# Cross-quadrant maxima by a TensorE transpose in some attention units, and side work of VectorE placed elsewhere

## The chip, the cores and the metric

One core of a Trainium2 chip. The metric is the device time of one execution in microseconds. The engines are called as the profile calls them: PE (TensorE matmul) with PEld (its weight loads), DVE (VectorE), ACT (ScalarE), POOL (GpSimd), SP (the queue that issues most DMAs).

## The reference

```python
x = A_x                                              # [1, 2048, 576]
sa, ca, ga, sb, cb, gb = (silu(c) @ w_mod) in six rows of 576
h = layernorm(x) * (1 + ca) + sa
q = (h @ wq) in 32 heads of 128                      # k, v: the last 512 cached keys, 16 heads, each used by 2 query heads
p = softmax(q @ k.T * 128**-0.5)
x = x + ga * ((p @ v) @ wo)
h = layernorm(x) * (1 + cb) + sb
x = x + gb * ((relu(h @ W_gate) * (h @ W_up)) @ W_down)   # 4608 hidden columns
```

All in float32. The kernel makes every large product out of two fp32r pieces per operand (a rounded "hi" and a remainder "lo"): hi*hi, hi*lo and lo*hi, so three matmuls for one.

## The kernel before

The program has two parts. The first, to about 1570 us, is attention in 128 **units**: one unit is one query head with one block of 512 queries (`UNITS` lists them; a key/value head `g` is visited for some query blocks after another). The second part is the gated MLP, with a seven-product scheme in place of eight; the change leaves it as it is.

The order of the instructions of PE, DVE, ACT and POOL is the order in which Python issues them (`manual_schedule`), and each engine works its list strictly in that order. The loop over `u` at the end of the function writes a unit out by hand. Around it stands a table `sched` of side steps, each with a time `10*u + k`: `run(u, k)` issues all steps up to that time, at place `k` of unit `u`. With such steps the layer norms of later query blocks, the loading and splitting of weights, the sums that make the six modulation rows, and the preparation of the MLP are spread over the units.

What one unit `u` does, in the order in which it stands:

- `s_half` (L543 to L545): 12 matmuls of keys times queries, 512 wide, into two PSUM tiles `s`. The third matmul of each group reads `qlo`, the low part of the projected queries. Behind each half DVE reduces the tile (`t`, L548): the largest score in every 32x32 block, transposed on the way.
- `max_pre` and `sum_pre` (L553, L558) bring the unit's maxima and the previous unit's sums of exponentials into a small tile `mxs`, 32 columns, where each of the four groups of 32 partitions ("quadrants") holds its own part.
- `turn`: the four quadrants are joined. Three DVE moves copy quadrants 1 to 3 to the first (L562, `mxs`), two reductions take the maximum and the sum over the four (L570), three moves copy the result back (L562, `both`).
- `qproj(u + 1)` (L467): 14 matmuls, the projection of the next unit's queries, into PSUM `qps`. A layer norm's transposes (L397, `lta` and `ltb`) may stand ahead of it.
- `max_bc` (L587): a DVE transpose spreads the maxima over 512 columns (`mb`); then `sum_inv` takes the reciprocal of the sums.
- `piece` (L683, `wo`): 12 matmuls of 288 columns of the output projection, into the one tile of the pool `psW`. A layer norm's transposes use the same tile, and DVE or ACT reads them out of it (L449, L443, L409).
- `pv_half(u - 1, 0)`, `exp_half` (DVE subtracts `mb` from `s`, L600; ACT takes exponentials and rounds, `hi`; POOL starts the sums, `ks` L606), `sum_bc(u - 1)` (L582, `rb`), `q_lo(u + 1)` (L525), `ksum_op` (`ks`: L618 on DVE, then L618 on POOL), `pv_half(u - 1, 1)`, another `piece`, `o_mul(u - 1)` (L664), and on POOL `lo_half` twice (`lo`, L612), which the next unit's `pv` needs.

The pool `psM` has two banks, given out in turn to `qps`, `pv` and a few transposes and sums. The pool `psS` has two tiles for `s`.

Side steps that the change touches are made by `prep(name, t, pr, gap)`: a load (`.l`) at an earlier place; for the output weights a gating (`.g`: DVE multiplies 128x576 weights by a modulation row, L264, both operands in SBUF); and the last step (`.c`) at `t`: the split into hi and lo, or, for the modulation rows, one multiply-add on DVE (`mod_step`, L120 and L122, `macc`).

Of the kernel before, what the change touches and what calls it, by code (L numbers as in the profile page):

```python
# [7 lines left out]
F32 = mybir.dt.float32  # L8
# [3 lines left out]
ALU = mybir.AluOpType  # L12
AX = mybir.AxisListType

P = 128
# [9 lines left out]
SCALE = float(P) ** -0.5  # L25
H2 = D // 2
SUM, MLP0 = 3, 8
NLAST = 5


@with_exitstack
def kernel(
# [13 lines left out]
    nc = tc.nc  # L46
# [10 lines left out]
    bp = ctx.enter_context(tc.tile_pool(name="bp", bufs=3))  # L57
    op = ctx.enter_context(tc.tile_pool(name="op", bufs=3))
# [6 lines left out]
    psM = psM_scope.__enter__()  # L65
# [3 lines left out]
    ident = cp.tile([P, P], F32, name="ident")  # L69
# [9 lines left out]
    mxs = cp.tile([P, 4, 32], F32, name="mxs")  # L79
    nc.vector.memset(mxs, 0.0)  # L80
    both = cp.tile([P, 32], F32, name="both")
# [52 lines left out]
    def prep_mod(j, t):  # L134
        st = {}

        def load():
            st["raw"] = xp.tile([P, 640], F32, tag="xm", name=f"wm{j}_{t}")
            nc.sync.dma_start(st["raw"][:, :D], wmod[j, :, t * D:(t + 1) * D])

        return load, lambda: mod_step(j, t, st["raw"][:, :D])
# [350 lines left out]
    NU = HKV * NQB * 2  # L492
# [3 lines left out]
    VIS = [(g, qbs) for qbs in ((0, 1), (2, 3)) for g in range(2)]  # L496
    VIS += [(g, (0, 1, 2, 3)) for g in range(2, HKV - NLAST)]
    VIS += [(g, (0, 1)) for g in range(HKV - NLAST, HKV)] + [(g, (2, 3)) for g in range(HKV - NLAST, HKV)]
    UNITS = [(g, qb, 2 * g + hh) for g, qbs in VIS for qb in qbs for hh in range(2)]
# [5 lines left out]
    def unit(u):  # L505
        return UNITS[u]
# [16 lines left out]
    def q_lo(u):  # L523
        qlo[u] = qp.tile([P, 512], F32R, tag="qlo", name=f"qlo{u}")
        nc.vector.scalar_tensor_tensor(qlo[u], qst.pop(u)[0], SCALE, qhi[u].bitcast(F32),  # L525
                                       op0=ALU.mult, op1=ALU.subtract)

    st_, t4, pt, hi_, lo_, bc, rb, rinv, ks_, pvps, done, o = ({} for _ in range(12))

    def by_sum(u):  # L530
        return 0 <= u < SUM
# [23 lines left out]
    def sum_pre(u):  # L555
        if by_sum(u):
            return
        nc.vector.tensor_reduce(mxs[:, 0, 16:], ks_.pop(u).rearrange("p (b j) -> p b j", j=32),  # L558
                                axis=AX.X, op=ALU.add, apply_transpose=True)

    def shift(dst, src):
        nc.vector.tensor_reduce(dst, src[:, :, None], axis=AX.X, op=ALU.max)  # L562

    def turn(u):
        for q in range(1, 4):
            shift(mxs[:32, q, :], mxs[32 * q:32 * q + 32, 0, :])
        for j, op in ((0, ALU.max), (1, ALU.add)):
            if u > SUM if j else u < NU:
                c = slice(16 * j, 16 * j + 16)
                nc.vector.tensor_reduce(both[:32, c], mxs[:32, :, c].rearrange("p q b -> p b q"),  # L570
                                        axis=AX.X, op=op)
        for q in range(1, 4):
            shift(both[32 * q:32 * q + 32, :], both[:32, :])

    def sum_inv(u):
        r = rinv[u] = sp.tile([P, 16], F32, tag="ri", name=f"ri{u}", bufs=1)
        nc.vector.reciprocal(r, both[:, 16:])
# [5 lines left out]
                            r[:, :, None].to_broadcast([P, 16, 32]))  # L583

    def max_bc(u):
        m = bp.tile([P, 512], F32, tag="bc", name=f"mb{u}")
        nc.vector.transpose(m.rearrange("p (b j) -> p b j", j=32),  # L587
                            both[:, :16, None].to_broadcast([P, 16, 32]))
        if u > SUM:
            sum_inv(u - 1)  # L590
        bc[u] = m
# [5 lines left out]
    def exp_half(u, h):  # L597
        t = st_.pop((u, h))
        p = pp.tile([P, 2, 512], F32, tag="p", name=f"p{u}_{h}")
        nc.vector.tensor_tensor(p, t, bc[u][:, None, :].to_broadcast([P, 2, 512]),  # L600
                                op=ALU.subtract)
        nc.scalar.activation(p, p, AF.Exp, bias=0.0, scale=1.0)  # L602
        pt[u, h] = p
        if h == 0 and not by_sum(u):
            ks_[u] = xp.tile([P, 512], F32, tag="xm", name=f"ks{u}")
            nc.gpsimd.tensor_tensor(ks_[u], p[:, 0, :], p[:, 1, :], op=ALU.add)  # L606
        if h and u:
            hi_half(u, 0)
# [11 lines left out]
    def pv_half(u, h, late=False):  # L620
        g, qb, hd = unit(u)
        if h == 0:
            pvps[u] = psM.tile([P, 512], F32, tag="mm", name=f"pv{u}")
        ps, v, a, b = pvps[u], vs[g], hi_[u, h], lo_[u, h]
        for j in range(2):
            kt = 2 * h + j
            nc.tensor.matmul(ps, v[:, kt, :], a[:, j, :], start=(kt == 0), stop=False)  # L627
            nc.tensor.matmul(ps, v[:, 4 + kt, :], a[:, j, :], start=False, stop=False)  # L628
            if not late:
                nc.tensor.matmul(ps, v[:, kt, :], b[:, j, :], start=False, stop=(kt == 3))  # L630
        for j in range(2 if late else 0):
            kt = 2 * h + j
            nc.tensor.matmul(ps, v[:, kt, :], b[:, j, :], start=False, stop=(kt == 3))
        if h:
            done[u] = pvps.pop(u)
# [707 lines left out]
    def step(name, t, fn, *args):  # L1343
        sched.append((t, len(sched), fn, args))
# [4 lines left out]
    def hook(q):  # L1349
        return 10 * (q // 4) + HOOK[q % 4]  # L1350

    def prep(name, t, pr, gap=2):
        q = 4 * (t // 10) + HOOK.index(t % 10)
        step(name + ".l", hook(q - gap), pr[0])
        if len(pr) > 2:
            step(name + ".g", t if t == 49 else hook(q - 1), pr[1])
        step(name + ".c", t, pr[-1])

    def setd(d, k, fn):
        def go():  # L1360
# [155 lines left out]
    for t, key, d, k in ((5, ("q", 0), wqs, 0), (8, ("k", 0), ks, 0), (12, ("q", 1), wqs, 1),  # L1516
                         (16, ("v", 0), vs, 0), (37, ("o", 0), wos, 0), (43, ("o", 1), wos, 1)):
        sk(t, key, d, k)
    live = {"q": wqs, "k": ks, "v": vs, "o": wos}
    early = range(HKV - NLAST + 1, HKV)  # L1520
    parks = {c: [w for g in early for w in weights(g, {x: {} for x in "qkvo"}) if w[0][0] in c]
             for c in ("q", "kv", "o")}
    seen, first = {0}, HKV - NLAST + 2
    for i in range(1, len(VIS)):
# [12 lines left out]
        seen.add(g)  # L1537
    for i in range(1, HKV - NLAST):
        B = 80 * i
        for c, t, gap, a in (("q", 16, 5, 0), ("kv", 24, 5, 1), ("o", 44, 6, 2)):  # L1540
            if parks[c] and i > a:
                key, d, pr = parks[c].pop(0)
# [1 line left out]
                sk(B + t + 9, key, d, key[1])  # L1544
    assert not any(parks.values())
    for i in range(15):
        prep(f"m{3 + i // 5}.{i % 5}", 109 + 30 * i - 10 * (i == 8), prep_mod(3 + i // 5, i % 5), 5)
    step("m3.pad", 238, mod_pad, 3)
    step("m4.pad", 388, mod_pad, 4)
    step("m3.col", 250, setd(mods, "b0", lambda: mod_col(3, 0.0)()))  # L1550
# [39 lines left out]
    for i in range(4):  # L1590
        m = 2 + 2 * i
# [79 lines left out]
    mlp = mlp_slots()  # L1671

    def last_unit():
        sum_inv(NU - 1)
        sum_bc(NU - 1)
        o_mul(NU - 1)
# [21 lines left out]
    t = 546  # L1698
    for s in ("P1", "P2", "P4", "P7", "P5", "P6", "P3"):
        for xx in range(2):  # L1700
            for fn in w_later(s, xx, (xp, "xm", 640)):
                step("w.l", t, fn)
                t = after(t + 8)
# [40 lines left out]
    def run(u, k):  # L1744
        t = 10 * u + k
        while sched and sched[-1][0] <= t:
            fn, args = sched.pop()[2:]
            fn(*args)
# [11 lines left out]
    for u in range(NU):  # L1760
        run(u, 0)
        if u > 1 and u % 2 == 0:
            o_hi(u - 2)
            o_lo(u - 2)
        s_half(u, 0)
        s_half(u, 1)
        max_pre(u)
        if u:
            sum_pre(u - 1)
        turn(u)  # L1770
        run(u, 1)
        if u + 1 < NU:
            qproj(u + 1, 0, 14)
        else:
            piece(at[10 * u + 1])
        if u == 1:
            hi_half(0, 0)
            hi_half(0, 1)
            lo_half(0, 0)
            lo_half(0, 1)  # L1780
        run(u, 2)
        if u + 1 == NU:
            pv_half(u - 1, 0, True)
        max_bc(u)
        if u + 1 < NU:
            q_hi(u + 1)
        run(u, 3)
        if 10 * u + 3 in at:
            piece(at[10 * u + 3])
        if u > 1 and u % 2:  # L1790
            o_hi(u - 2)
            o_lo(u - 2)
        run(u, 4)
        if by_sum(u - 1):
            pv_sums(u - 1)
        elif u + 1 == NU:
            pv_half(u - 1, 1, True)
        elif u:
            pv_half(u - 1, 0)
        flush(pend_act)  # L1800
        exp_half(u, 0)
        flush()
        run(u, 5)
        if u == 0:
            q_lo(1)
        exp_half(u, 1)
        if u > SUM:
            sum_bc(u - 1)
        if 0 < u < NU - 1:
            q_lo(u + 1)  # L1810
        if by_sum(u - 1):
            sums_inv(u - 1)
        ksum_op(u, 0)
        ksum_op(u, 1)
        run(u, 6)
        if SUM < u < NU - 1:
            pv_half(u - 1, 1)
        if 10 * u + 6 in at:
            piece(at[10 * u + 6])
        run(u, 7)  # L1820
        if u:
            o_mul(u - 1)
        flush()
        run(u, 8)
        if u + 1 == NU:
            flush(pend_act)
        if u:
            hi_half(u, 1)
        flush(pend_act)
        if u:  # L1830
            lo_half(u, 0)
            lo_half(u, 1)
        run(u, 9)
# [56 lines left out]
```

## Time and profile before

| | |
|---|---|
| median of 3 runs | 2844.81 us (2843.04 to 2846.78) |
| the profiled execution | 2843.61 us, its span 2841.8 us |
| PE busy | 2812.6 us, 99% of the span, 15054 matmuls |
| DVE busy | 2321.3 us, 82% |
| POOL busy | 2216.8 us, 78% |
| ACT busy | 1415.6 us, 50% |

The share of busy time hides stages: DVE is at 92% while attention runs and at 61% to 81% afterwards. PE's busy time is that of pipelined matmuls, whose ends are modelled, so a row's length is not what it costs: the distance to the next row's start is. An idle time in front of a matmul is shown with what ended it. A weight load is issued ahead of its matmul, so the same wait also shows, a little longer, in the rows of PEld.

### The profile page before, as it was taken

What the parts mean: (1) busy time and instruction counts of PE and PEld (TensorE: products, weight loads), DVE (VectorE), ACT (ScalarE), POOL (GpSimd) and SP (SyncE); (2) the same over time, 40 slices, a digit from 0 to 9 for tenths busy, and PEclk for the clock granted to TensorE, in tenths of its full rate; (3) what the DMA queues carried; (4) which work ended last, traced back from release to release, by engine and by line L of the source; (5) the groups of instructions that cost most, each with busy time, mean ns of one, the idle gap of its engine ahead of it and who ended that gap; (6) DMA issues with size and microseconds to landing.
All of it is one profiled execution on the core that took longest, in us unless ns stands there. A gap on an engine that the chain in (4) does not pass through costs nothing.

```text
span 2841.8 us, 42016 instructions
## 1 busy us (share of the span) xinstructions
PE 2812.6 (99%) x15054; PEld 2451.2 (86%) x15054; DVE 2321.3 (82%) x3866; ACT 1415.6 (50%) x2020; POOL 2216.8 (78%) x1596
## 2 busy tenths in 40 slices
PE   8999999999999999999999999999999999999999
PEld 7788888888888888888888888888888888888888
DVE  8999999999989999888999877778777566666666
ACT  6766666666666666666656433333333222222220
POOL 6878888888899989777778766777887577777773
PEclk9999999999999999999999999999999999999999
DMA  6322132223232223322244465666777844444443
GB/s 236 106 91 89 62 101 91 85 68 110 101 103 86 93 63 136 99 76 79 73 139 138 151 210 204 228 230 224 259 252 278 316 156 155 156 156 153 151 150 137
DMA packets 166881, 411.43 MB, mean 145 GB/s; under 512 B 15728, under 2 KB 62576, under 8 KB 166672
## 3 DMA queue, kind: packets, MB, share of 16 engines
q1 hardware_dynamic: 132768, 287.65, 31.4%
q10 hardware_dynamic: 33904, 121.09, 10.8%
q8 instruction: 119, 1.95, 0.3%
q14 instruction: 90, 0.74, 0.1%
HBM read 276.53 MB, written 160.73 MB: 154 GB/s over the span
## 4 chain that ended last, share of the span: by engine, by line
PE 64%; DVE 5%; POOL 2%; ACT 1%; issue 1%; DMA 0%; SPq 0%; ACTq 0%; POOLq 0%; DVEq 0%
PE gh_P L1159 28%; PE md L683 9%; PE mf L767 6%; PE wo L683 6%; PE qps L467 5%; PE s L545 2%; PE s L544 2%; PE s L543 2%; PE pv L630 1%; PE pv L628 1%; PE pv L627 1%; DVE t L548 1%; POOL lo L612 1%; POOL ks L606 1%; DVE p L600 1%
## 5 line engine op out<-in xcount | busy, mean ns | idle before, releaser
L612 POOL TENSOR_TENSOR lo<-p,hi 128x1024 fp32r<-128x1024 f32 x256 | 623.1, 2455 | 0.5
L1159 PE MATMUL gh_P<-hop_B,wop 128*128 128x512 f32 x1470 | 352.9, 390 | 0.0
L548 DVE TRANSPOSE_TENSOR_REDUCE t<-s 128x32 f32<-128x1024 f32 x256 | 311.9, 1235 | 42.1 <-PE s L545 34.7
L1159 PEld LDWEIGHTS gh_P<-hop_B,wop 128*128 128x128 f32 x1470 | 270.0, 188 | 50.6 <-DVE q L1196 0.2
L600 DVE TENSOR_TENSOR p<-s,mb 128x1024 f32<-128x1024 f32 x256 | 299.9, 1209 | 0.3
L602 ACT ACTIVATE p<-p 128x1024 f32<-128x1024 f32 x256 | 264.1, 1056 | 58.8 <-DVE p L600 57.1
L467 PE MATMUL qps<-hTa,wA 128*128 128x512 f32 x1176 | 281.8, 390 | 1.8 <-DVE hTa L443 1.4
L1159 PE MATMUL gh_P<-hop_T,wop 128*128 128x512 f32 x1138 | 282.8, 390 | 0.0
L683 PE MATMUL wo<-woga,ohi 128*128 128x288 f32 x1344 | 271.9, 295 | 5.0 <-DVE hTa L449 3.9
L467 PEld LDWEIGHTS qps<-hTa,wA 128*128 128x128 f32 x1176 | 220.2, 188 | 49.0 <-DVE hTa L443 1.8
L595 ACT CAST hi<-p 128x1024 fp32r<-128x1024 f32 x256 | 257.2, 1039 | 0.0
L683 PE MATMUL md<-wogb,hhi 128*128 128x288 f32 x1280 | 257.2, 294 | 0.0
L618 POOL TENSOR_TENSOR ks<-ks,p 128x512 f32<-128x512 f32 x125 | 166.8, 1334 | 107.3 <-DVE ks L618 104.4
L1159 PEld LDWEIGHTS gh_P<-hop_T,wop 128*128 128x128 f32 x1138 | 208.8, 188 | 39.3
L683 PEld LDWEIGHTS wo<-woga,ohi 128*128 128x128 f32 x1344 | 224.3, 188 | 20.3 <-DVE hTa L449 5.6
L521 ACT ACTIVATE qhi<-qps 128x512 fp32r<-128x512 f32 x128 | 76.4, 597 | 330.8 <-PE qps L467 327.5
L606 POOL TENSOR_TENSOR ks<-p 128x512 f32<-128x512 f32 x125 | 162.4, 1299 | 100.9 <-ACT p L602 99.2
L683 PEld LDWEIGHTS md<-wogb,hhi 128*128 128x128 f32 x1280 | 212.2, 188 | 10.6 <-DVE q L1184 0.2
L694 DVE TENSOR_TENSOR acc<-md,acc 128x576 f32<-128x576 f32 x160 | 120.1, 754 | 104.7 <-PE md L683 103.4
L1159 PE MATMUL gh_P<-hy_T,wop 128*128 128x512 f32 x618 | 200.6, 391 | 0.0
L683 PE MATMUL wo<-woga,olo 128*128 128x288 f32 x672 | 198.7, 296 | 0.4 <-POOL olo L672 0.3
L672 POOL TENSOR_TENSOR olo<-rb,ohi 128x512 fp32r<-128x512 f32 x128 | 166.6, 1302 | 32.2 <-ACT ohi L668 31.9
(322 smaller groups left out, 7510.3 us busy)
## 6 DMA issues: line engine op xcount, KB each, us to landing
wop<-wk_P SPq DMA_DIRECT2D x133, 640.0 KB
wk_P<-wop ACTq DMA_DIRECT2D x119, 640.0 KB
wr<-wlay SPq DMA_DIRECT2D x68, 384.0 KB
againq<-akq SPq DMA_DIRECT2D x22, 640.0 KB
againo<-ako SPq DMA_DIRECT2D x18, 576.0 KB
rogb<-wd SPq DMA_DIRECT2D x36, 288.0 KB
rwA<-wq SPq DMA_DIRECT2D x32, 320.0 KB
roga<-wo SPq DMA_DIRECT2D x32, 288.0 KB
```

The costliest lines, as they stand in the source:

```text
L467: return [lambda i=i, a=a, b=b: nc.tensor.matmul(ps, a, b, start=(i == 0), stop=(i == n - 1)) for i, (a, b) in enumerate(ops)]
L548: nc.vector.tensor_reduce(t4[u][:, 2 * h:2 * h + 2, :].rearrange("p k b -> p (k b)"), t.rearrange("p k (b j) -> p (k b) j", j=32), axis=AX ...
L595: nc.scalar.copy(hi_[u, h], pt[u, h])
L600: nc.vector.tensor_tensor(p, t, bc[u][:, None, :].to_broadcast([P, 2, 512]), op=ALU.subtract)
L602: nc.scalar.activation(p, p, AF.Exp, bias=0.0, scale=1.0)
L606: nc.gpsimd.tensor_tensor(ks_[u], p[:, 0, :], p[:, 1, :], op=ALU.add)
L612: nc.gpsimd.tensor_sub(lo_[u, h], pt[u, h], hi_[u, h].bitcast(F32))
L618: eng.tensor_tensor(ks_[u], ks_[u], pt[u, 1][:, j, :], op=ALU.add)
L672: nc.gpsimd.tensor_sub(olo[u], o.pop(u), ohi[u].bitcast(F32))
L683: nc.tensor.matmul(ps[:, half, :H2], a[:, sl], w[b][:, cs], start=(n == 0 and seed is None), stop=(n == 5), skip_group_check=seed is not None)
L767: nc.tensor.matmul(ps[:, j, :H2], x[:, sl], w[:, c:c + H2], start=i == 0, stop=i == 2)
L1159: nc.tensor.matmul(ps, a, c, start=s not in ("P2", "P3") and i == 0, stop=i == len(ops) - 1, skip_group_check=True)
```

## The change

- A unit with `u < 15` or `u >= 110` (`by_turn`, and the closing step of the last unit) joins the quadrants in another way. DVE makes one transpose of the 32 columns, repeated four times, inside each quadrant (`mt`, 128x128, in the first columns of the tile that later holds `mb`); PE transposes that 128x128 tile through the identity into a PSUM tile `qm` (`spread`, right behind the projection of the next unit and ahead of the first `piece`); DVE reduces `qm` over the quadrants, once for the maxima and once for the sums (`quads`). The eight small operations of `join` are gone there. `qm` is a third tile in the rotation of `psM`. The other 95 units keep `join`.
- In every unit `q_lo(u + 1)` now stands ahead of `sum_bc(u - 1)`, with a place 5.5 between them for side steps.
- All gatings but one (`t == 49`) and the 15 multiply-adds of the modulation rows move to that place 5.5.

```diff
+TURNS = (15, 110)
...
+    def by_turn(u):
+        return u < TURNS[0] or u >= TURNS[1]
...
-    def turn(u):
+    def join(u):
         for q in range(1, 4):
             shift(mxs[:32, q, :], mxs[32 * q:32 * q + 32, 0, :])
...
+    def turn(u):
+        if not by_turn(u):
+            join(u)
+            return
+        bps[u] = psM.tile([P, 512], F32, tag="mm", name=f"qm{u}")
+        bc[u] = bp.tile([P, 512], F32, tag="bc", name=f"mb{u}")
+        mt[u] = bc[u][:, :P]
+        nc.vector.transpose(mt[u].rearrange("p (a b) -> p a b", a=4),
+                            mxs[:, 0, None, :].to_broadcast([P, 4, 32]))
+
+    def spread(u):
+        if not by_turn(u):
+            return
+        nc.tensor.transpose(bps[u][:, :P], mt.pop(u), ident)
+
+    def quads(u, k):
+        return bps[u][:, :P].rearrange("p (a k b) -> p k b a", a=4, k=2)[:, k]
+
+    def sum_add(u):
+        if by_turn(u + 1):
+            nc.vector.tensor_reduce(both[:, 16:], quads(u + 1, 1), axis=AX.X, op=ALU.add)
...
     def max_bc(u):
-        m = bp.tile([P, 512], F32, tag="bc", name=f"mb{u}")
+        if by_turn(u):
+            nc.vector.tensor_reduce(both[:, :16], quads(u, 0), axis=AX.X, op=ALU.max)
+        if u > SUM:
+            sum_add(u - 1)
+        m = bc[u] if by_turn(u) else bp.tile([P, 512], F32, tag="bc", name=f"mb{u}")
...
-            step(name + ".g", t if t == 49 else hook(q - 1), pr[1])
-        step(name + ".c", t, pr[-1])
+            step(name + ".g", t if t == 49 else (t - 6) // 10 * 10 + 5.5, pr[1])
+        step(name + ".c", t + shift, pr[-1])
...
-        prep(f"m{3 + i // 5}.{i % 5}", 109 + 30 * i - 10 * (i == 8), prep_mod(3 + i // 5, i % 5), 5)
+        prep(f"m{3 + i // 5}.{i % 5}", 109 + 30 * i - 10 * (i == 8), prep_mod(3 + i // 5, i % 5), 5, -3.5)
...
     def last_unit():
+        spread(NU)
+        sum_add(NU - 1)
         sum_inv(NU - 1)
...
             pv_half(u - 1, 0, True)
+        spread(u)
         max_bc(u)
...
         exp_half(u, 1)
+        if 0 < u < NU - 1:
+            q_lo(u + 1)
+        run(u, 5.5)
         if u > SUM:
             sum_bc(u - 1)
-        if 0 < u < NU - 1:
-            q_lo(u + 1)
```

Three places show it. First DVE in unit 7, one in which a layer norm's transposes are read out (`hTa`); before:

```order
L548 TENSOR_REDUCE t_7_1604<-s_1_1606 128x32
L553 TENSOR_REDUCE mxs<-t_7_1604 128x16
L558 TENSOR_REDUCE mxs<-ks_1545 128x16
L562 TENSOR_REDUCE mxs<-mxs 32x32 x3
L570 TENSOR_REDUCE both<-mxs 32x16 x2
L562 TENSOR_REDUCE both<-both 32x32 x3
L449 TENSOR_TENSOR hTa_4_1634<-lta_0_1624,hTa_0_1633 128x512
L587 STREAM_TRANSPOSE mb_1660<-both 128x512
```

and now:

```order
L549 TENSOR_REDUCE t_7_1583<-s_1_1585 128x32
L554 TENSOR_REDUCE mxs<-t_7_1583 128x16
L559 TENSOR_REDUCE mxs<-ks_1524 128x16
L586 STREAM_TRANSPOSE mb_1596<-mxs 128x128
L450 TENSOR_TENSOR hTa_4_1608<-lta_0_1598,hTa_0_1607 128x512
L613 TENSOR_REDUCE both<-qm_1595 128x16
L599 TENSOR_REDUCE both<-qm_1595 128x16
L617 STREAM_TRANSPOSE mb_1596<-both 128x512
```

Eight small operations stood between the reductions of the scores and the reading of the norm's transposes; one transpose stands there now, and the two reductions of `qm` come behind.

Second PE in the same unit, from the end of the projection of the next unit's queries (now; before, the row of `qm` is not there and all else is the same):

```order
L468 MATMUL qps_1618<-hTa_7_1461,againq_1254 128x512
L468 MATMUL qps_1618<-hTa_8_1407,againq_1254 128x512 x2
L592 MATMUL qm_1595<-ident,mb_1596 128x128
L713 MATMUL wo_3_1642<-woga_1014,ohi_1117 128x288 x2
L713 MATMUL wo_3_1642<-woga_1014,olo_1119 128x288
```

One transpose stands between the projection and the output projection's piece, and it reads what DVE writes into `mb`.

Third DVE in unit 43, the one place where a gating and a multiply-add fell together (`p_1` is the second half of the scores less the maxima); before:

```order
L600 TENSOR_TENSOR p_1_6320<-s_1_6244,mb_6277 128x1024
L582 STREAM_TRANSPOSE rb_6325<-ri_6279 128x512
L525 SCALAR_TENSOR_TENSOR qlo_6327<-qps_6262,qhi_6281 128x512
L618 TENSOR_TENSOR ks_6318<-ks_6318,p_1_6320 128x512
L664 TENSOR_TENSOR rb_6325<-pv_6305,rb_6325 128x512
L122 SCALAR_TENSOR_TENSOR macc_5977<-wm_1_6201,sT,macc_5977 128x576
L264 TENSOR_TENSOR roga_6232<-roga_6232,mrow_1005 128x576
L548 TENSOR_REDUCE t_44_6374<-s_0_6367 128x32
```

and now:

```order
L630 TENSOR_TENSOR p_1_6275<-s_1_6199,mb_6232 128x1024
L526 SCALAR_TENSOR_TENSOR qlo_6280<-qps_6217,qhi_6236 128x512
L265 TENSOR_TENSOR roga_6188<-roga_6188,mrow_992 128x576
L123 SCALAR_TENSOR_TENSOR macc_5896<-wm_1_6157,sT,macc_5896 128x576
L608 STREAM_TRANSPOSE rb_6284<-ri_6234 128x512
L648 TENSOR_TENSOR ks_6273<-ks_6273,p_1_6275 128x512
L694 TENSOR_TENSOR rb_6284<-pv_6260,rb_6284 128x512
L549 TENSOR_REDUCE t_44_6329<-s_0_6322 128x32
```

Both side operations moved from behind `o_mul` (the second `rb` row), just ahead of the next unit's `t`, to a place behind `qlo` and ahead of the first `rb`, `ks` and `o_mul`.

More of the change, by code (lines that the diff above doesn't have):

```diff
@@ L526, in q_lo @@
                                        op0=ALU.mult, op1=ALU.subtract)
-    st_, t4, pt, hi_, lo_, bc, rb, rinv, ks_, pvps, done, o = ({} for _ in range(12))
+    st_, t4, mt, pt, hi_, lo_, bc, rb, rinv, ks_, pvps, done, o, bps = ({} for _ in range(14))
     def by_sum(u):
@@ L1350, in hook, with prep @@
         return 10 * (q // 4) + HOOK[q % 4]
-    def prep(name, t, pr, gap=2):
+    def prep(name, t, pr, gap=2, shift=0):
         q = 4 * (t // 10) + HOOK.index(t % 10)
```

## Prediction

> **What bounds the kernel now.** I read the page's first part, then stages by time, then who PE's weight loads wait for in each stage, and last single units in order of time. The sum is made against the profiled execution, 2843.6 us, 1.2 us (0.04%) under the median of the runs.
>
> ```profile
> PE 2812.6 (99%) x15054; PEld 2451.2 (86%) x15054; DVE 2321.3 (82%) x3866; ACT 1415.6 (50%) x2020; POOL 2216.8 (78%) x1596
> ```
>
> Busy time, per engine. PE is the bound; what can be won are the stretches in which it waits. The next view cuts the span (columns: length, then busy time and instructions of PE, PEld, DVE, ACT, POOL, granted clock, DMA share, GB/s): units 0 to 14, 15 to 109, 110 to 126.
>
> ```profile
> 24.35:219.47 195.12, 183.73 (x923) 154.39 (x924) 178.71 (x348) 131.47 (x184) 157.11 (x105) 0.98 0.34 119
> 219.47:1357.32 1137.85, 1132.69 (x5916) 980.26 (x5915) 1039.42 (x1951) 766.83 (x1048) 975.61 (x598) 1.00 0.28 91
> 1357.32:1570.44 213.12, 208.33 (x1096) 178.39 (x1095) 201.59 (x386) 135.19 (x183) 168.31 (x104) 1.00 0.37 121
> ```
>
> PE idles 11.4 us in the first stage, 5.2 and 4.8 in the next two; DVE is at 91% to 95% in all three. The change touches hardly anything behind them. Who PE's weight loads waited for, first stage, then second, then third (total, times, longest):
>
> ```profile
> PEld wo L683 <- DVE hTa L449: 5.6, 4, 2.4
> PEld sums L643 <- ACT woga L218: 2.6, 1, 2.6
> PEld s L545 <- DVE qlo L525: 2.0, 3, 1.3
> PEld qps L467 <- DVE hTa L443: 1.8, 1, 1.8
> ...
> PEld s L545 <- DVE qlo L525: 8.6, 17, 2.0
> PEld s L543 <- DVE p L600: 1.2, 1, 1.2
> ...
> PEld wo L683 <- DVE lfb L409: 4.4, 4, 1.1
> PEld s L545 <- DVE qlo L525: 3.5, 5, 1.6
> ```
>
> Nearly all are waits for something that DVE does late. A load runs ahead of its matmul, so of each a part is not lost: a wait of 1.1 us there stands below as one of 0.67 at the matmul, which with about 0.27 for refilling PE costs 0.94. I take 0.15 off each. Now a unit without a stall (unit 9), PE then DVE:
>
> ```profile
> 150.75 3.34 PE L467 MATMUL qps<-hTa,againq 128*128 128x512 f32 x14
> 153.93 0.42 PE L683 MATMUL wo<-woga,ohi 128*128 128x288 f32 x2
> ...
> 149.59 2.61 DVE L548 TRANSPOSE_TENSOR_REDUCE t<-s 128x32 f32<-128x1024 f32 x2 [0.63 <-PE s L545]
> 152.24 0.27 DVE L553 TENSOR_REDUCE mxs<-t 128x16 f32<-128x64 f32 x1
> 152.43 0.70 DVE L558 TRANSPOSE_TENSOR_REDUCE mxs<-ks 128x16 f32<-128x512 f32 x1
> 153.16 0.55 DVE L562 TENSOR_REDUCE mxs<-mxs 32x32 f32<-32x32 f32 x3
> 154.22 0.56 DVE L562 TENSOR_REDUCE both<-both 32x32 f32<-32x32 f32 x3
> 154.82 0.71 DVE L587 STREAM_TRANSPOSE mb<-both 128x512 f32<-128x512 f32 x1
> 161.42 2.61 DVE L548 TRANSPOSE_TENSOR_REDUCE t<-s 128x32 f32<-128x1024 f32 x2 [0.50 <-PE s L545]
> ```
>
> A clean unit takes 11.83 us (161.42 less 149.59). The join takes DVE 1.66 us, from 153.16 to 154.82.
>
> **The change, part by part.** *The new join.* The transpose inside the quadrants is not in the trace. Its bounds are a 32x32 move, 0.18 us (0.55 for three), and the 512-wide transpose, 0.71; it has a quarter of the latter's columns, so I take 0.22. It would end at 153.38, and PE leaves the projection at 153.93: in a clean unit PE does not wait, with 0.55 us to spare. PE then transposes, its end and a semaphore take some 0.3 us, two reductions (64 elements per partition as at L553, bounds 0.18 and 0.27 each) 0.5: `mb` starts at about 154.8, as before. So the chain of a clean unit is no shorter; DVE has 0.9 us less to do and waits for PE instead. What gains are things queued behind the join.
>
> *PE's own cost.* Eight transposes of a norm:
>
> ```profile
> 1397.90 1.03 PE L397 MATMUL ltb<-ident,xnb 128*128 128x128 f32 x8
> 1398.69 1.17 PE L467 MATMUL qps<-hTa,againq 128*128 128x512 f32 x4
> ```
>
> 0.79 us from start to start, 0.10 each, and a little for the change of shape: 0.115 for one alone, 34 of them: **+3.9 us**. Nothing hides it.
>
> *Units 113 to 117 and 5 to 8, a norm read out behind the join:*
>
> ```profile
> 1401.96 0.81 DVE L409 TENSOR_SCALAR lfb<-ltb,mcol,mcol 128x512 f32<-128x512 f32 x1
> 1402.82 0.53 PE L683 MATMUL wo<-againo,ohi 128*128 128x288 f32 x2 [0.67 <-DVE lfb L409]
> ```
>
> The piece needs the PSUM tile that `lfb` reads. `lfb` comes 1.44 us earlier (1.66 less 0.22), more than the 0.67. Each of the four late ones cost 0.67 and about 0.27 for refilling: **-3.75**. Units 5 to 8 have the same, 5.6 us at the loads, 5.0 at the matmuls, and half-speed clock behind the longest:
>
> ```profile
> 31.16:34.57 3.41, 1.52 (x11) 1.31 (x12) 3.24 (x8) 3.41 (x8) 2.41 (x3) 1.00 0.59 222
> 34.57:37.98 3.41, 3.41 (x9) 2.61 (x9) 2.24 (x3) 3.38 (x5) 3.33 (x4) 0.50 0.45 140
> 96.00:99.42 3.42, 1.45 (x9) 0.99 (x8) 3.20 (x13) 0.76 (x2) 3.42 (x3) 1.00 0.88 303
> 99.42:102.83 3.41, 3.41 (x13) 3.04 (x13) 3.38 (x8) 1.68 (x2) 2.36 (x3) 0.50 0.18 69
> 580.65:584.06 3.41, 1.82 (x8) 1.19 (x7) 3.20 (x6) 3.40 (x4) 1.75 (x2) 1.00 0.13 49
> ```
>
> A stretch of 3.41 us with PE busy 1.45 or 1.52 was followed by one at clock 0.50, which costs 1.7 us; one with 1.82 (the stage it lies in has a clock of 1.00) was not. In unit 5 (the third and fourth rows) the wait, the longest, shrinks by 1.4 us, so the clock should hold. But DVE is full there, 3.20 and 3.38 of 3.41 us in the last-but-two and last-but-one rows: PE comes earlier than DVE can follow. DVE gains 0.9 us a unit, PE's part is 1.4 and 1.7; I put the difference, with what unit 5 keeps, at 1.0 us of waiting at unit 6's new transpose and 1.8 at the pieces. 5.0 + 1.7 - 2.8: **-3.9**.
>
> *Units 0 and 1.* The second unit's scores wait for the first's `p`, which waits for the join: `mb` comes 0.6 us sooner (a join without sums, 1.4, less 0.22, 0.3 and one reduction), the stretch ahead of 34.57 gets busier than 1.82, the clock holds: 0.6 + 1.7, **-2.3**.
>
> *Units 1 to 4.* `hTa` L443, `qlo` and `sums` all stand behind a join, 6.4 us at the loads in five waits, 5.6 at the matmuls. DVE cannot be ahead of PE here: it gains 0.9 a unit at most, and what PE wins in unit 1 beyond that, unit 2 gives back as a wait for its transpose. Of units 1 to 3 that leaves 2.7 as the most, and 0.6 I take off for what is late next (`wo` behind `sums`): **-2.1**, bounds 0 and 5.6.
>
> *Units 111, 112 and 123 to 126, `qlo`.* 3.5 us at the loads, 2.8 at the matmuls, and the reductions of unit 111:
>
> ```profile
> 1376.02 0.70 DVE L558 TRANSPOSE_TENSOR_REDUCE mxs<-ks 128x16 f32<-128x512 f32 x1
> ```
>
> `qlo` moves ahead of `rb` (L582, as long as `mb`, 0.7) and gains from the join, 1.5 in all, so the waits go. But unit 111's scores then end 1.5 us earlier, at about 1372.1, and PE leaves the projection 3.2 later, at 1375.3; DVE, only 0.8 earlier, ends its new transpose at 1376.1. With refilling 1.0 comes back: **-1.8**. The last unit's transpose stands on PE right behind its last `pv` and waits a little: **+0.3**.
>
> *The middle, 95 units.* No PE transposes. 9.8 us at the loads in 18 waits, 7.1 at the matmuls, are one thing: a gating or multiply-add at the end of a unit makes DVE late for the next. POOL's `lo` over the whole program (mean of one, 2455 ns), and the worst place, units 43 to 45:
>
> ```profile
> L612 POOL TENSOR_TENSOR lo<-p,hi 128x1024 fp32r<-128x1024 f32 x256 | 623.1, 2455 | 0.5
> ...
> 566.51 1.30 POOL L606 TENSOR_TENSOR ks<-p 128x512 f32<-128x512 f32 x1 [0.55 <-ACT p L602]
> 567.02 0.65 DVE L525 SCALAR_TENSOR_TENSOR qlo<-qps,qhi 128x512 fp32r<-128x512 f32 x1
> 567.85 0.69 DVE L618 TENSOR_TENSOR ks<-ks,p 128x512 f32<-128x512 f32 x1 [0.18 <-POOL ks L606]
> 568.62 1.29 POOL L618 TENSOR_TENSOR ks<-ks,p 128x512 f32<-128x512 f32 x1 [0.81 <-DVE ks L618]
> 569.06 1.47 DVE L122 SCALAR_TENSOR_TENSOR macc<-wm,sT,macc 128x576 f32<-128x576 f32 x1
> 569.87 2.92 POOL L612 TENSOR_TENSOR lo<-p,hi 128x1024 fp32r<-128x1024 f32 x1
> 570.45 2.96 DVE L264 TENSOR_TENSOR roga<-roga,mrow 128x576 f32<-128x576 f32 x1
> 582.65 0.50 PE L545 MATMUL s<-qlo,kv 128*128 128x512 f32 x1 [1.59 <-DVE qlo L525]
> ```
>
> L264 ends 0.6 us behind the end of the POOL operation that was under way when it came, L122 too: where both sources lie in SBUF, DVE waits for POOL. At the new place it waits for POOL's `ks` L606 instead and ends about 0.6 us behind it, so DVE's `ks`, `o_mul` and the next `t` move by 1.2 us in place of 1.47 or 2.96, and `qlo` stands ahead of all this and of `rb`. But for the longest two, the waits are 0.41 on average at the loads (6.6 in 16), and `qlo` alone now comes 0.63 earlier in its unit: nothing is left of them. The longest two, 3.2 at the loads, 2.9, lie here: DVE is 2.3 us less late, and I leave 0.9: **-6.2**, bounds 0 and 7.1. Behind the moved operations now stands POOL's `ks`, delayed 1.2 us less the 0.47 by which `lo` was stretched (2.92 less 2.455). POOL idles 0.81 us ahead of it, so a little should reach a `pv` that waits for `lo`: **+0.3**, bounds 0 and the slower rival below. The loads of the gated weights are asked for some 7 us ahead instead of 10; no wait for them is in the trace, and I add nothing.
>
> *Sum:* 3.9 - 3.75 - 3.9 - 2.3 - 2.1 - 1.8 + 0.3 - 6.2 + 0.3 = -15.55: 2843.6 less that is **2828 us**.
>
> **Rivals.** *The clock does not rise with the shorter waits.* The Trainium skill, "TensorE: Matmul & The Clock Gate", section "Why this matters for your kernels", has the clock drop only for idle gaps of about 3 us, one idle window. The rows above speak against it, with drops behind windows half busy. By that rule the shorter waits would win no clock. If both half-speed stretches stay, 3.4 us are not won: 2831.
>
> *PE waits at every new transpose.* If the DVE transpose takes the upper bound of 0.71, the 0.55 us of a clean unit is just used up, and the some eight late units wait 0.5 longer: +4, 2832. Each PE wait also costs the refilling.
>
> *The moved gatings hold up POOL* (slower). 45 operations delay POOL's sums and `lo`. The Trainium skill, "SBUF — State Buffer", section "Who interferes with whom", says that a DVE instruction with two SBUF inputs and a GpSimd one that reads SBUF lock each other out for the whole instruction; the trace agrees, with the 0.6 us above. If each of the 45 pushed a `pv` by 0.7 us, with 0.27 of refilling, that is +44: 2872. It decides from 16 of 45 on (15.55 / 0.97). Against it: POOL idles 0.81 us ahead of L618 and so has some room. If only ten places do it, where POOL also splits output weights, 2838.
>
> *The change does less than it says*: DVE so full around the norms that every win returns at the next transpose. Then the first and last stages give only their clock and PE pays 3.9: 2838.
>
> **How the numbers follow.** My sum, with 2822 to 2833 as its own range, 0.55; clock or slow transpose (2831 to 2836) 0.17; one half lost (2836 to 2842) 0.13; nothing won 0.08; slower by POOL 0.07. 0.2% is 5.7 us, about what a measurement of this kernel can tell from no change; of the half-lost cases a little falls within it. Faster 0.83, same 0.10, slower 0.07. Range 2819 to 2841: below for waits on POOL and DMA that I left standing.
>
> **What would show it.** Right: no `wo <- hTa` or `wo <- lfb` row, `s <- qlo` gone from the second stage, no clock of 0.50 between 24 and 1600 us, new rows of `qm` on PE with waits only in units 2, 6 and 111, the stages shorter by about 7, 6 and 3 us, the MLP unchanged. Wrong: `qm` waiting in clean units, `pv <- POOL lo` in many, or `roga` waiting for a DMA.

## The result, and the profile after

| | before | after |
|---|---|---|
| median | 2844.16 us (6 runs, 2843.04 to 2846.78) | 2825.97 us (6 runs, 2825.70 to 2826.43) |
| ratio | | 0.9939, 95% interval 0.9928 to 0.9949 |
| profiled execution, its span | 2843.61, 2841.8 us | 2826.43, 2824.7 us |

Faster by 18 us; the forecast was 2828 with a range of 2819 to 2841. The two profiled executions are 17.2 us apart. First the busy times of the changed kernel, from the page:

```profile
PE 2808.3 (99%) x15088; PEld 2452.2 (87%) x15088; DVE 2297.0 (81%) x3696; ACT 1412.8 (50%) x2020; POOL 2198.0 (78%) x1596
```

PE has its 34 transposes more, DVE 170 operations and 24 us less. The same stretches by time as before (units 0 to 14, 15 to 109, 110 to 126, and from unit 127 to the end; columns as in the prediction):

```profile
23.93:211.55 187.62, 183.00 (x938) 152.83 (x938) 165.05 (x273) 131.41 (x184) 156.48 (x105) 1.00 0.35 123
211.55:1345.79 1134.24, 1129.82 (x5916) 981.64 (x5915) 1042.87 (x1951) 766.15 (x1048) 958.30 (x598) 1.00 0.28 91
1345.79:1555.29 209.50, 209.06 (x1113) 179.65 (x1112) 186.44 (x302) 134.97 (x184) 169.24 (x104) 1.00 0.38 123
1555.29:2824.70 1269.41, 1265.05 (x6980) 1118.99 (x6978) 885.11 (x1126) 367.88 (x588) 906.74 (x779) 1.00 0.57 198
```

The first three are shorter by 7.5, 3.6 and 3.6 us ("about 7, 6 and 3" was forecast). The last was 1271.36 us before and is 1.95 shorter, where the forecast had it 0.3 longer. The startup is 0.4 shorter, with no changed code in it. The clock is 1.00 in all four: no stretch at 0.50 as at 34 and 99 us before is left in them. Who PE waited for (total, times, longest); the first five rows are of the first stage, the next three of the second, the last of the third:

```profile
PE s L544 <- DVE p L630: 1.1, 1, 1.1
...
PE lta L398 <- DVE acc L724: 0.6, 1, 0.6
PE sums L673 <- DVE both L613: 0.5, 1, 0.5
...
PE qm L592 <- DVE mb L586: 0.3, 1, 0.3
PE wo L713 <- DVE hTa L450: 0.2, 1, 0.2
...
PE wo L713 <- POOL woga L220: 1.8, 4, 0.8
...
PE wo L713 <- DMA againo<-ako: 1.2, 2, 0.8
PE wo L713 <- POOL olo L702: 0.7, 1, 0.7
...
PE qm L592 <- DVE mb L586: 0.4, 2, 0.2
```

The waits for the reads of a norm behind the join (`hTa`, `lfb`) are gone or down to 0.3 or less. `qlo` is gone from the second stage, and in its place stands POOL: the cut of the output weights (`woga` L220) and of the head's output (`olo`). The new `qm` makes PE wait in units 0, 110, 111 and in the closing join, 0.2 to 0.3 us each.

The new join in a unit without a wait (unit 9), PE and DVE in order of time:

```profile
140.84 2.61 DVE L549 TRANSPOSE_TENSOR_REDUCE t<-s 128x32 f32<-128x1024 f32 x2
142.00 3.34 PE L468 MATMUL qps<-hTa,againq 128*128 128x512 f32 x14
144.40 0.31 DVE L586 STREAM_TRANSPOSE mb<-mxs 128x128 f32<-128x128 f32 x1
145.18 0.27 PE L592 MATMUL qm<-ident,mb 128*128 128x128 f32 x1
145.49 0.22 DVE L613 TENSOR_REDUCE both<-qm 128x16 f32<-128x64 f32 x1 [0.77 <-PE qm L592]
145.63 0.21 DVE L599 TENSOR_REDUCE both<-qm 128x16 f32<-128x64 f32 x1
145.76 0.70 DVE L617 STREAM_TRANSPOSE mb<-both 128x512 f32<-128x512 f32 x1
```

DVE's transpose takes 0.31 us (0.22 was taken) and ends 0.47 us before PE is free, so PE does not wait; DVE does, 0.77 us. `mb` starts 4.92 us behind the first `t` (5.23 before). The unit takes 11.95 us instead of 11.83: PE's price is 0.12 per transpose.

### The profile page after: what moved, and what is told of

It is laid out like the page before. It is cut to its first block, busy times and chain, and to the rows that moved or that the text cites. A ratio compares the mean times of both kernels' runs of the same rounds, so it can differ in the third digit from the quotient of the medians.

```text
span 2824.7 us, 41922 instructions
## 1 busy us (share of the span) xinstructions
PE 2808.3 (99%) x15088; PEld 2452.2 (87%) x15088; DVE 2297.0 (81%) x3696; ACT 1412.8 (50%) x2020; POOL 2198.0 (78%) x1596
## 3 DMA queue, kind: packets, MB, share of 16 engines
q8 instruction: 119, 1.95, 0.3%
## 4 chain that ended last, share of the span: by engine, by line
PE 91%; POOL 3%; DVE 2%; ACT 2%; issue 1%; DMA 1%; ACTq 0%; POOLq 0%; DVEq 0%
PE gh_P L1189 28%; PE wo L713 13%; PE qps L468 13%; PE md L713 9%; PE mf L797 6%; PE s L546 4%; PE s L545 4%; PE s L544 4%; PE pv L658 3%; PE pv L657 3%; PE pv L660 3%; POOL lo L642 1%; PE gu L1189 1%; POOL olo L702 1%; ACT p L632 0%
## 5 line engine op out<-in xcount | busy, mean ns | idle before, releaser
L642 POOL TENSOR_TENSOR lo<-p,hi 128x1024 fp32r<-128x1024 f32 x256 | 610.7, 2407 | 0.5
L713 PE MATMUL md<-wogb,hlo 128*128 128x288 f32 x640 | 188.8, 295 | 0.0
```

The source lines that it names most:

```text
L642: nc.gpsimd.tensor_sub(lo_[u, h], pt[u, h], hi_[u, h].bitcast(F32))
L713: nc.tensor.matmul(ps[:, half, :H2], a[:, sl], w[b][:, cs], start=(n == 0 and seed is None), stop=(n == 5), skip_group_check=seed is not None)
```

## The experiments

Lengths in us of the three stages, and from unit 127's first score matmul to the end of the span, each from its kernel's profiled execution; the medians are those of the timed runs. Each ratio goes by the kernel before as it was timed beside that run, with a median of 2843.15, 2843.96 or 2843.88 us (2844.16 for the changed kernel).

| kernel | units 0-14 | 15-109 | 110-126 | from 127 | median | ratio to before, 95% interval |
|---|---|---|---|---|---|---|
| before | 195.1 | 1137.9 | 213.1 | 1271.4 | 2844.2 | |
| after | 187.6 | 1134.2 | 209.5 | 1269.4 | 2826.0 | 0.9939 (0.9928 to 0.9949) |
| the join alone | 187.7 | 1137.7 | 209.2 | 1268.9 | 2831.1 | 0.9958 (0.9945 to 0.9970) |
| join and q_lo | 187.5 | 1134.4 | 209.2 | 1269.0 | 2826.1 | 0.9936 (0.9922 to 0.9950) |
| gatings at 6 | 187.4 | 1131.9 | 209.2 | 1268.9 | 2823.2 | 0.9930 (0.9918 to 0.9942) |
| the moves alone | 195.2 | 1139.7 | 212.4 | 1271.5 | 2844.2 | 1.0003 (0.9994 to 1.0012) |
| the moves, SP's row put back | 195.3 | 1136.8 | 212.5 | 1271.4 | 2839.4 | 0.9983 (0.9974 to 0.9992) |
| the join in all units | 187.5 | 1145.3 | 208.5 | 1269.0 | 2836.4 | 0.9977 (0.9968 to 0.9986) |
| gatings at 6, fewer joins | 186.7 | 1132.0 | 208.5 | 1272.7 | 2824.6 | 0.9930 (0.9917 to 0.9943) |
| the same, closing join new | 186.7 | 1132.1 | 208.5 | 1270.7 | 2823.8 | 0.9926 (0.9914 to 0.9939) |
| the same, unit 127 too | 186.6 | 1132.3 | 208.5 | 1270.2 | 2823.6 | 0.9926 (0.9913 to 0.9940) |

**The join alone.**

```diff
-        step(name + ".g", t if t == 49 else (t - 6) // 10 * 10 + 5.5, pr[1])
+        step(name + ".g", t if t == 49 else hook(q - 1), pr[1])
-        prep(..., prep_mod(3 + i // 5, i % 5), 5, -3.5)
+        prep(..., prep_mod(3 + i // 5, i % 5), 5)
...
         exp_half(u, 1)
-        if 0 < u < NU - 1:
-            q_lo(u + 1)
-        run(u, 5.5)
         if u > SUM:
             sum_bc(u - 1)
+        if 0 < u < NU - 1:
+            q_lo(u + 1)
```

> Only the new join in units 0 to 14 and 110 to 127; q_lo, gatings and multiply-adds at their old places. If the parts add up (my theory): the first stage keeps most of its gain (187 to 190 us long), the middle is as in the kernel before (1137.5 to 1138.5), the third keeps the gain at the lfb pieces but not the q_lo waits of units 123 to 126 (210.5 to 212): about 2832 us. Rival, the moves alone carry the change: the third and first stages within 1 us of before and PE's 34 transposes unpaid, about 2843. Second question: whether the passage to the MLP, 1.95 us shorter after the change, owes that to the join (then it is 1269.4 here) or to the moves (then 1271.4).

The first and third stages have their whole gain, the third even without the earlier q_lo; the middle has none; the shorter stretch from unit 127 on is the join's as well. So by the medians the join is worth 12.0 us of the 18 and the moves 5.2, and these lie in the middle (3.3 to 3.5 between the profiled executions; that of the join alone was the fastest of its five).

**The moves alone.**

```diff
-TURNS = (15, 110)
+TURNS = (0, 1000)
```

> No TensorE transposes at all; q_lo ahead of sum_bc, gatings and multiply-adds at 5.5. My theory: the middle is as after the change, 1134 us, 3.6 under before; the first stage within 1 us of before, 194 to 195, with both half-clock stretches left in it; the third 1 to 2 us under before through q_lo: about 2837 us. Rival, the moves help only where the join also does (the early and late stages were full on DVE): the first stage over 195 and the third at 213, about 2840.

Both theories missed the whole. The first and third stages stay within 0.7 us of before, near to what the rival said; but the middle is 1.8 us longer than before, although PE, DVE, ACT and POOL have there the order of the changed kernel. Its waits in the middle, PE's and then, from 219 to 320 us, those of ACT and DVE:

```profile
PE wo L713 <- ACT wo L746: 2.6, 1, 2.6
PE wo L713 <- POOL woga L220: 1.9, 4, 0.9
...
ACT kv L219 <- DMA rkv<-kv: 8.6, 1, 8.6
DVE roga L265 <- DMA roga<-wo: 4.6, 1, 4.6
```

But for the first row PE waits much as in the changed kernel. That one is a chain: ACT stands 8.6 us at the keys and values that have not landed, behind it stands its copy into `wo`, and PE waits 2.6 us and runs behind it at a granted clock of 0.51 (246.0 to 249.5 us, matmuls of 0.63 us in place of 0.39). SP's queue shows why, in this kernel and then in the changed one:

```profile
226.73 0.33 SPq L489 DMA_DIRECT2D againo<-ako  x1
227.11 3.62 SPq L1599 DMA_DIRECT2D wlay<-wg  x2
230.85 5.24 SPq L241 DMA_DIRECT2D rkv<-kv  x1
```

```profile
196.63 0.59 SPq L1599 DMA_DIRECT2D wlay<-wg  x1
218.84 0.33 SPq L489 DMA_DIRECT2D againo<-ako  x1
219.21 0.59 SPq L1599 DMA_DIRECT2D wlay<-wg  x1
219.92 2.97 SPq L241 DMA_DIRECT2D rkv<-kv  x1
```

SP's queue is not written out by hand, and one row has slipped: a copy of MLP weights (`wlay`), which used to go out 22 us ahead of `againo`, now stands behind it. `againo` waits for PE, so both copies go out together and the load of keys and values follows 3 us later, behind 256 KB more. The load of the gated weights (`roga`) stands farther back in the same queue, and a gating waited 4.6 us for it.

**The moves alone, with SP's row put back.** One step is given an earlier time, which changes no row of PE, DVE, ACT or POOL:

```diff
-        step("lay", ... else 140 + 7 * (i - len(lay0)),
+        step("lay", ... else 140 + 7 * (i - len(lay0)) - 3 * (i == len(lay0)),
```

> The kernel with the moves alone, and on SP's queue one row put back: a copy that rewrites MLP weights (wlay) goes out ahead of the load of the parked output weights (againo), as in the changed kernel, where the moves alone had put it behind, so that the next keys and values (rkv) were asked for 3 us later and landed 5 us later. Theory: that one row cost the moves their gain; without it the middle is as after the change, 1134.3 us in place of 1139.7, and the whole about 2838.8. Rival: the moves need the join (the middle starts late), and the middle stays at 1137 to 1139.7, the whole at 2841 or more.

The median is 2839.35, as the theory had it: the moves are worth 4.6 us without the join and 5.2 with it (2831.1 less 2826.0), and the slipped row cost 4.8. The wait for the keys and values is back near the changed kernel's 3.0 us:

```profile
ACT kv L219 <- DMA rkv<-kv: 3.2, 1, 3.2
```

The middle of the profiled execution is longer than forecast; that execution was the slowest of its eleven (2842.25), and it holds a wait of its own, with what came of it:

```profile
653.44 0.76 DVE L265 TENSOR_TENSOR roga<-roga,mrow 128x576 f32<-128x576 f32 x1 [4.85 <-DMA akq<-wA]
655.47 1.29 POOL L648 TENSOR_TENSOR ks<-ks,p 128x512 f32<-128x512 f32 x1 [4.65 <-DVE ks L648]
659.16 0.50 PE L660 MATMUL pv<-lo,kv 128*128 128x512 f32 x1 [1.20 <-POOL lo L642]
```

A gating at 5.5 stood 4.85 us at a DMA, and POOL's sums and `lo` were late behind it. That unit (51) took 15.45 us, 12.75 in the changed kernel: about the 2.6 us by which the middle is longer than there. What was loading is not settled by this row: the DMA named is another tile's.

**The join and q_lo.** The edit is that of the join alone with q_lo left at its new place.

> The new join and q_lo ahead of sum_bc; gatings and multiply-adds at their old places. Theory (the prediction's): q_lo coming 0.65 us earlier in its unit does away with nearly all q_lo waits by itself, and without the moved operations POOL is not held up: middle 1133 to 1135 us against 1137.7 with the join alone and 1134.25 with all, in all 2824 to 2828. Rival: the waits come from the gatings at the unit's end, which make DVE late for the next t whatever stands where within the unit: middle 1136.5 to 1138, in all 2829 to 2831.

q_lo alone brings all of the middle's 3.3 us; with the gatings and multiply-adds moved as well the middle is the same within 0.2. The waits of PE's loads for `qlo` in the middle, first with the join alone, then with q_lo moved as well:

```profile
PEld s L546 <- DVE qlo L526: 8.7, 17, 2.0
...
PEld s L546 <- DVE qlo L526: 1.6, 2, 1.4
```

In 14 units of the join alone that have no other wait, loads wait 0.3 to 0.6 us for `qlo`, and the unit is longer than 11.83 by that wait less about 0.15, which was the rule of the prediction. With q_lo moved six of the seven waits that are left, the shortest too short for the row above, are 0.2 or less.

**Gatings at 6.** What then do the moved gatings do?

```diff
-        step(name + ".g", t if t == 49 else (t - 6) // 10 * 10 + 5.5, pr[1])
+        step(name + ".g", t if t == 49 else (t - 6) // 10 * 10 + 6, pr[1])
-        prep(..., prep_mod(3 + i // 5, i % 5), 5, -3.5)
+        prep(..., prep_mod(3 + i // 5, i % 5), 5, -3)
```

> The changed kernel with gatings and multiply-adds one place later, behind the sums of exponentials (DVE's ks and POOL's ks) in place of ahead of them. My theory: at 5.5 they delay DVE's ks, behind it POOL's ks and lo, and so POOL's cut of the output weights (waits wo <- POOL woga and olo, 3 to 4 us of the middle with refilling). At 6 POOL's ks is asked for before they begin, so these waits shrink and the middle is 2 to 3 us shorter: 1131.5, in all 2823. Rival: DVE then ends behind POOL's second ks, o_mul and the next unit's t are late, and the q_lo waits come back: middle 1136 or more, 2828 or more. Third: POOL's waits have another cause (POOL is simply full in those units), no difference, 2826.

The middle is 2.3 us shorter than after the change and the whole 2823.18: the first theory. The gatings of the output weights, and POOL's second `ks` behind them (count, then total and mean, then idle time before it and who ended it), first at 5.5, then at 6; with the join alone, at the old places, the means are 1260 and 1333 and POOL's idle time 105.6:

```profile
L265 DVE TENSOR_TENSOR roga<-roga,mrow 128x576 f32<-128x576 f32 x30 | 44.3, 1476 | 3.2 <-DMA akq<-wA 2.0 <-DMA roga<-wo 1.0
...
L648 POOL TENSOR_TENSOR ks<-ks,p 128x512 f32<-128x512 f32 x125 | 162.0, 1296 | 139.6 <-DVE ks L648 127.2 <-PE s L546 8.4 <-ACT acc L722 2.4
```

```profile
L265 DVE TENSOR_TENSOR roga<-roga,mrow 128x576 f32<-128x576 f32 x30 | 23.3, 775 | 0.0
...
L648 POOL TENSOR_TENSOR ks<-ks,p 128x512 f32<-128x512 f32 x125 | 180.6, 1445 | 105.4 <-DVE ks L648 103.8 <-ACT hi L625 1.6
```

At 5.5 POOL idles 34 us more ahead of `ks`, some 0.77 for each of the 44 moved operations (29 gatings, 15 multiply-adds), and everything on POOL behind it is late by that, `lo` and then the weights' cut. At 6 that idle time is gone, and a gating takes half as long, because it now begins first. One of each, at about the same unit; at 5.5:

```profile
735.45 1.32 POOL L220 TENSOR_TENSOR kv<-rkv,kv 128x512 fp32r<-128x512 f32 x1
735.75 1.64 DVE L265 TENSOR_TENSOR roga<-roga,mrow 128x576 f32<-128x576 f32 x1
```

and at 6:

```profile
738.26 0.75 DVE L265 TENSOR_TENSOR roga<-roga,mrow 128x576 f32<-128x576 f32 x1
738.42 1.74 POOL L648 TENSOR_TENSOR ks<-ks,p 128x512 f32<-128x512 f32 x1 [0.81 <-DVE ks L648]
```

The gating that comes second ends 0.62 us behind POOL's operation; the one that comes first takes 0.75, and POOL's 1.74 in place of some 1.29. It is so nearly everywhere: of the 29 moved gatings 27 began behind an operation of POOL at 5.5, and 26 of these ended 0.61 or 0.62 us behind it; at 6 all 29 began first and took 0.75. The Trainium skill, "SBUF — State Buffer", section "Who interferes with whom", says that the order of issue, not the operation, decides who blocks; these rows agree. At 6 no gating waits at a DMA either; at 5.5 two did, 2.0 and 1.0 us.

**The join in all units.**

```diff
-TURNS = (15, 110)
+TURNS = (1000, 0)
```

> The new join in all 128 units. PE pays 95 more transposes of about 0.115 us, 10.9 us. If DVE's 0.9 us a unit wins nothing in the middle: 2837. If it removes the waits that are left there (3.7 us): 2833. If PE waits at the new transposes of units with a gating (DVE late by 0.5 in some 45 of them): 2845 or more. I take 2837.

The middle is 11.1 us longer, 95 times 0.117: PE pays for each transpose and wins nothing net there. The waits at POOL go, but `qm` brings its own (over the whole program):

```profile
PE qm L592 <- DVE mb L586: 2.4, 8, 0.4
```

**The clock by itself.** In the kernel before, PE is given idle work in unit 5, which nothing reads:

```diff
+        if u == 6:
+            for i in range(14):
+                nc.tensor.matmul(ps[:, :P], ident, ident, start=True, stop=True)
         for f in qst[u][1][lo:hi]:
             f()
```

> The kernel before, with 14 idle 128x128 matmuls on TensorE ahead of one projection in unit 5, at about 98 us, where it waits for hTa (they run inside that wait and their result is not used). Theory: the clock falls to 0.50 for a stretch of 3.41 us when TensorE was busy for less than about half of the stretch before; filled, the drop at 99.42 us is gone and the first stage is 1.7 us shorter, 193.4. Rival, only a gap of some 3 us without any work lowers the clock: then the fill changes nothing there, or the drop has another cause and stays (195.1 or a little more).

Units 1, 5 and 6 before (columns as above, the clock third from the end):

```profile
34.36:49.17 14.81, 13.45 (x55) 10.49 (x55) 11.60 (x20) 12.64 (x17) 12.03 (x9) 0.88 0.50 191
89.66:106.55 16.89, 14.92 (x77) 12.69 (x75) 15.95 (x32) 9.98 (x14) 12.80 (x9) 0.90 0.32 114
106.55:120.38 13.83, 13.08 (x74) 11.14 (x71) 13.29 (x28) 12.14 (x19) 11.95 (x10) 1.00 0.11 43
```

and with the idle work:

```profile
34.18:47.76 13.58, 12.16 (x54) 9.21 (x55) 11.59 (x20) 12.65 (x17) 12.04 (x9) 1.00 0.54 208
88.23:104.43 16.20, 16.20 (x104) 14.54 (x103) 15.25 (x30) 9.54 (x14) 12.28 (x8) 1.00 0.34 119
104.43:119.04 14.61, 13.32 (x74) 11.07 (x72) 14.16 (x30) 12.62 (x20) 12.49 (x10) 1.00 0.10 40
```

The drop in unit 5 is gone, as the theory wanted. But the 0.69 us that unit 5 wins, unit 6 gives back (0.78): DVE was no earlier, and PE waits for it one unit later. That says little of the price, since the idle work, 3.05 us long where the wait had been 1.97, also put off the projection. The drop in unit 1 is gone too, with no change there, and the 1.2 us by which the first stage is shorter (193.9) lie in that unit. This was one execution, of 2841.59 us.

The traces say more of what decides it. The stretches at 0.50 lie on a grid of 3.41 us, which begins elsewhere in each execution: in the kernel before they start at 34.57, 99.42 and, behind the last matmuls, 2840.32 us, 19 and 822 steps from the first. From the first scores on, in the traces of all twelve kernels, each step of the grid in which PE was busy 1.52 us or less was followed by one at 0.50, and none in which it was busy 1.56 us or more. With the idle work, counted back from the stretch at its end, a step of the grid cuts unit 1's idle time in two:

```profile
29.92:33.33 3.41, 2.25 (x16) 1.60 (x14) 3.15 (x11) 3.41 (x8) 2.40 (x3) 1.00 0.91 325
33.33:36.74 3.41, 2.52 (x10) 1.70 (x11) 3.26 (x4) 3.38 (x6) 3.41 (x4) 1.00 0.31 99
```

That fits: before, the step from 31.16 us held 1.52. No run moved the grid by itself, so this is a regularity and not an experiment.

**Fewer joins.** With the gatings at 6, the new join in units 0 to 8 and 110 to 118; then for the closing join too (`or u == 128`); then for unit 127 as well (`or u >= 127`):

```diff
-        return u < TURNS[0] or u >= TURNS[1]
+        return u < 9 or 110 <= u < 119
```

> As with the gatings at place 6, and the new join only in units 0 to 8 and 110 to 118, the closing join by moves too: 16 transposes on TensorE fewer, 1.9 us. If those 16 joins win nothing: 2821.3 us. If the closing ones carry the shorter passage to the MLP (1269.4 us against 1271.4 with moves): the passage is 1271.4 again and the whole 2823; with the q_lo waits of units 123 to 126 back as well, 2824 to 2825. I take 2823.

> Gatings at place 6; the new join in units 0 to 8 and 110 to 118 and for the closing join of the last unit, which gates6_fewer had made by moves; units 9 to 109 and 119 to 127 by moves. If the closing join carries the shorter passage: from unit 127 on it is 1266.9 us to the end of the span or less (gates6_fewer 1268.8 or more, gatings at 6 alone 1265.0) and the whole 2822.3. If unit 127's own join carries it, no change against gates6_fewer: 2824.5.

> As gates6_close, with unit 127 by the new join as well: 15 transposes on TensorE fewer than with gatings at 6 alone. The first and third stages as in gates6_fewer (186.7 and 208.5 us, 1.4 together under those with gatings at 6), the passage as there (1265.0 from unit 127 to the end of the last matmul): 2823.18 less 1.4 is 2821.8. Rival: unit 126's late end (its join by moves) makes unit 127 late and the passage keeps part of the 3.8 us: 2823 or more.

The two stages win 1.4 us, where 14 transposes at 0.12 cost 1.7. From unit 127 on it is 3.8 us longer, of which the closing join brings back 2.0 and unit 127's own 0.5. The expectations count up to the last matmul, 3.8 us before the span's end. The remaining 1.3 us are the rival of the last one, a lateness from the units before, seen at the copy into `wo` in that stretch:

```profile
PE wo L713 <- ACT wo L746: 0.8, 1, 0.8
```

So what units 119 to 126 save on PE (0.7) is lost behind them. None of this is clearly different from the gatings at 6 with all 34 joins, 2823.18 (2823.06 to 2823.78), which is faster than both kernels, than the changed one by 0.1%. Giving up the joins of units 9 to 14 alone, worth 0.7 by their stage, was not tried.

## Why the prediction was right, and where not

The forecast was 2 us too high; its mechanism held (PE waited for what DVE did late, and most of these waits went), and two terms were off, by some 2.3 us each. That these two cancel is luck; what is left of the miss is small differences in other terms. Two of the rivals can be set aside: PE waits more than 0.15 us at only 4 of the 34 new transposes, 0.9 us in all; and the clock did rise with the shorter waits. The prediction counts 45 moved operations; there are 44, which hardly changes the price of the slower rival.

- *PE's price:* 0.12 in a clean unit for 0.115. Right.
- *Units 5 to 8, -3.9:* these four took 58.35 us before and take 54.56, with 0.46 for their transposes a gain of 4.25. The waits at `hTa` are gone but for 0.2. What was left did not stand at unit 6's new transpose, as written, but one place ahead, at the tile that the norm's transposes use (`lta <- DVE acc`, 0.6): PE waits at the first thing that a late DVE still owes it. The half-clock row is gone; whether its 1.7 us was a gain of its own there is doubtful, since in the experiment on the clock the next unit gave it back.
- *Units 0 and 1, -2.3:* 24.82 us before, 22.50 now, with 0.23 for two transposes -2.55. Right in size, not in all its parts. Unit 0 has its 0.6. Unit 1 has 1.95 in place of 1.7, and by the one execution without a drop there the clock was worth some 1.2 of it. The drop is gone in every kernel with the join, where no step of the grid in units 0 and 1 has PE busy for less than 1.97 us (that grid is told under the clock experiment).
- *Units 2 to 4:* 40.49 before, 38.25 now, -2.6 with the transposes, where -2.1 stood.
- *Units 113, 114, 116 and 117, `lfb`:* 0.84 us shorter each with the transpose in it, -3.8 for -3.75. Units 110 to 112 and 119 to 126 together 1.8 without the transposes, as forecast; but it was the join that did it (209.2 with the join alone), not q_lo's place, to which the step gave a part.
- *The middle, -6.2 and +0.3:* -3.6 in place of -5.9. The step that failed is "**+0.3**" for POOL behind the moved operations: with the 2.3 us that place 6 wins back, it was some 2.6. The waits for `qlo`, some 6 us at the matmuls, went as forecast, all of them. But a gating at 5.5 is not 1.2 but 1.48 us long on average, POOL's 0.81 us of idle time was not room (POOL was in time only because DVE was), and the lateness came out at `wo`, through the cut of the weights and `olo`, not at `pv`. PE waits there 2.5 us in five places and refills after each. The slower rival had named this mechanism, and it was there in kind, at a small part of its price.
- *The loads of the gated weights, nothing added:* wrong in small. A gating waited twice at a DMA, 2.0 and 1.0 us on DVE, once ahead of a PE wait of 0.65 (`roga` at a DMA had been named as a sign of a wrong forecast), and 4.6 and 4.85 us in the two kernels with the moves alone.
- *Behind unit 127, +0.3:* -1.95. The step took the closing transpose alone, and overlooked that before the change that stretch had waits behind the old joins (`wo` for ACT's copy and DVE's `acc`, `pv` for `lo`), which have gone. The runs put 2.0 on the closing join, and 1.8 on unit 127's and those ahead of it. These waits in the kernel before, from unit 127 to 1700 us:

```profile
PE wo L683 <- ACT wo L716: 0.4, 1, 0.4
PE wo L683 <- DVE acc L694: 0.4, 1, 0.4
PE pv L633 <- POOL lo L612: 0.3, 1, 0.3
```

## What to carry to other kernels

Cost a moved operation by what stands behind it on its engine, and then by who waits for that: where another engine idles just ahead of the place, ask whether that idle time is room or already the wait for the same engine. Where an operation and another engine's hold each other up over their source memory, as the gatings and POOL's did here, try the place where it begins first. And where one queue's order is left to a scheduler, compare that queue's order too: here a row that slipped on SP cost as much as the moves had won.

## What was not expected of the hardware

- The same 128x576 product on DVE took 0.75 us where it began ahead of POOL's operation, and 1.26 and 1.48 us on average at places where it often began behind one.
- A DMA of keys and values that went out 3 us later, behind a copy of 256 KB, landed over 5 us later and cost 4.8 us of the whole.
- The granted clock fell to 0.50 in unit 1 in one execution of the kernel before and not in another with the same code there; the busy share of the 3.41 us step ahead tells them apart in all twelve traces, and the length of the gap does not (one of 2.22 us at 68 us before, cut by a step of the grid, had no drop; one of 1.69 us at 33 us had).
- The executions of the changed kernel lie within 0.7 us of each other; those of the kernel before, 2843.04 to 2846.78, within 3.7.
